# The router's logits of the values with the router weights stationary in three column groups

## The chip, the cores and the metric

One core of a Trainium2 chip runs the whole program. The time is what the device takes for one execution, in microseconds (us). TensorE is PE in the profile (PEld is its weight loads), VectorE is DVE, ScalarE is ACT, GpSimd is POOL, SyncE (which issues most DMAs) is SP.

## The reference

Three stages follow each other. (1) Attention in 16 heads (2 batches of 8) with 768 rows of 64 values, where a row attends only to the keys that have its own hash of six sign bits. (2) The 1536 rows of 512 values go through a mixture of 8 experts: each row goes to the expert with the largest logit, up to a capacity, and comes back weighted by its softmax probability. (3) A dense pair of layers with a hard swish between them. Cut to what matters here:

```
attn = softmax(where(mask, q @ k.T / 8, -1e9));  a = attn @ v          # 16 heads
x = a, heads side by side                                              # 1536 x 512
logits = x @ w_gate                                                    # 1536 x 8
e = argmax(logits);  gate = softmax(logits)[e]
y = relu(x @ w1[e]) @ w2[e] * gate
out = (h * clip(h + 3, 0, 6) / 6) @ w_out,  h = y @ w_in
```

## The kernel before

**How the logits come about.** The kernel doesn't form `x @ w_gate`. For each head it multiplies the values with that head's 64 rows of `w_gate` first, and appends the 8 columns that come out (a high and a low float16 half) to the values. The attention product then yields the 64 outputs and that head's share of the 8 logits at once. The function `vgate(r)` makes these columns for the pair of heads 2r and 2r+1, so it runs eight times, r = 0 to 7. Below, "product r" is its work on PE.

**What product r does.** The tile `vt` (loaded by `load_vt`, L526, one buffer) holds the values of the pair transposed: 128 partitions (two heads by 64) by 768 rows. For each of the six blocks of 128 rows, the block of `vt` is the stationary operand and the 16 columns of the weights (two heads by 8) are the moving one (L537). The result has the rows on the partitions. The program shows each such float32 product as two loads and two matmuls, so a pair has 12 of each. DVE then makes the two halves for each head (L546 and L547), into the tile `vh`.

**The loop.** The attention runs as 96 steps k, six for a head (one for each block of 128 keys), software-pipelined: step k makes the scores of block k on PE (L445, L446), their exponentials on ACT (L447), the float16 halves of block k-2 (L455 on ACT or L457 on DVE, L461 mostly on POOL), and the row maxima of block k+8 (L428 on PE, then two reductions of 384 columns on DVE, L431; the tile pool behind them has three banks of PSUM). In each odd step PE also multiplies two blocks of exponentials with the values (L473 to L475, 36 matmuls, the lines of `psv`). Every engine works through its instructions in the order in which the program text emits them.

**Small work between the steps.** All else hangs in a table of due times. `at(k, f)` puts a function at time k; `spread(k, gen, d)` runs a generator part by part, at k, k+d, k+2d and so on. Within step k, whatever is due up to k-0.5 is emitted ahead of the step's own work, and whatever is due up to k behind it; parts due at the same place go in order of their times. The table `Q` holds the times. `vgate` has two empty parts ahead of its matmuls, so they stand two parts after its start.

**One bank for the small products.** `misc()` hands out one PSUM bank (pool `ps_x`, one buffer) to everything small: the hash bits of the heads (`bits`, four matmuls of 32 columns each into four column groups, L401, and then the signs on DVE, L390), the scale of the values (`vscale`, L569 to L606, which in its first call also takes the maximum of the router weights, L571, and scales them, L605), the router's own counts, and `vgate`. A new user waits until the last reader of the one before is done.

**Around it.** SP issues the DMAs in the order of the program: loads of heads, copies of their halves into the operand tiles, the hash bits (L386), `vt`. After the loop come the routing (mostly small DVE work in a row), the experts (L1038, L1065) and the dense layers (L1287, L1314).

Of the kernel before, what the change touches and what calls it, by code (L numbers as in the profile page):

```python
# [9 lines left out]
F32 = mybir.dt.float32  # L10
# [9 lines left out]
P = 128  # L20
# [3 lines left out]
NC = S // P  # L24
# [3 lines left out]
KD = DM // P  # L28
E = 8
# [34 lines left out]
def moe_attention_kernel(ctx, tc, qk, v, vt, pj, wg, w1, w2, win, wout, out, cap):  # L64
    nc = tc.nc
    pe, act, dve, pool, sp = nc.tensor, nc.scalar, nc.vector, nc.gpsimd, nc.sync
# [16 lines left out]
    def persist(shape, dt, name):  # L83
        return const.tile(shape, dt, tag=name, name=name)
# [3 lines left out]
    ident = persist([P, P], F32, "ident")  # L88
# [6 lines left out]
    iota_s = persist([P, NS], F32, "iota_s")  # L95
    tokid = persist([P, NS], F32, "tokid")
    rank8 = persist([P, E], F32, "rank8")
    wg_sb = persist([P, KD, 2, E], F32, "wg_sb")
    isw = persist([P, 1], F32, "isw")
    lg = persist([P, B, NC, E], F32, "lg")  # L100
    ids = persist([P, E, NW], I32, "ids")
# [197 lines left out]
                )  # L299


    Q = {'v': (-3.25, -4.75, -1.75, -2.25), 'vg': (-4.5, -4.75), 'vgd': 1, 'pr': (-13.0, -12.75, -12.0, -12.5), 'prd': 0.6, 'b0': 7.75, 'b': 1.75, 'bd': 0.5, 'vm0': (8.0, 8.25, 10.75, 13.0), 'vm': (-0.5, 4.75, 7.0, 12.25), 'vs': 13.25, 'pa': 1.5, 'ev': 0.5, 'lvt': -5.0, 'v4': (2.0, 3.75, 4.0, 16.25), 'vg0': (1.85, -4.4, 7.75), 'p2': 3.5, 'lr': (0, 3, 1.5, 4.5), 'lv': 5.5, 'vsd': 0.75, 'ac': (0, 0, 2, 6, 7, 8, 9, 10), 'hd': (3, 5, 17), 'hn': (1, 3, 2, 0, 2, 0, 0, 0), 'ap': (0,), 'h0': (7,), 'hl': (4, 7, 10), 'l0': (), 'll': (1,), 'ht': (6, 3, 7, 6, 3, 2)}


    HT = Q["ht"]
# [1 line left out]
    with ExitStack() as actx:  # L307
# [220 lines left out]
        def vgate(r):  # L528

            sw = sw_t[r // 2]  # L530
            t = vt_t.pop(r)
            yield
            yield
            ps = misc(f"psg{r}")
            w = wg_sb[:, r % KD].rearrange("p h e -> p (h e)")
            for j in range(NC):
                pe.matmul(  # L537
                    ps[:, j * 2 * E : (j + 1) * 2 * E], t[:, j * P : (j + 1) * P], w, start=True, stop=True
                )
            yield  # L540
            ps = ps[:, 0 : NC * 2 * E].rearrange("p (c h e) -> p c h e", h=2, e=E)
            for hh in range(2):
                h = 2 * r + hh
                t = vh(h)
                o, ol = hh * D, VA + hh * D
                dve.tensor_scalar(out=t[:, :, o : o + E], in0=ps[:, :, hh], scalar1=sw, scalar2=None, op0=ALU.mult)  # L546
                dve.scalar_tensor_tensor(  # L547
                    out=t[:, :, ol : ol + E], in0=ps[:, :, hh], scalar=sw, in1=t[:, :, o : o + E],
                    op0=ALU.mult, op1=ALU.subtract,
                )  # L550
                yield
# [68 lines left out]
        def unmatched(r):  # L620

            b, k = divmod(r, KD)
            rows = rows_of(r)
            n = 2 * NC * D
            vt = pr.tile([P, S], F32, tag="r", name=f"uv{r}").rearrange("p (h c d) -> p h c d", h=2, c=NC)
            sp.dma_start(out=vt.rearrange("p h c d -> p (h c d)"), in_=v[:, r * n : (r + 1) * n])
            last = r == NH // 2 - 1
            if not last:
                x = pr.tile([P, S], F32, tag="r", name=f"ux{r}").rearrange("p (c d) -> p c d", c=NC)
                sp.dma_start(out=x, in_=rows)  # L630
            m = pt.tile([P, S], F32, tag="pf", name=f"um{r}", bufs=4)
            ps = misc(f"psu{r}")
            for c in range(NC):
                pe.matmul(ps[:, 0:P], ones, vt[:, :, c], start=c == 0, stop=c == NC - 1)
            act.activation(m[:, 0:P], ps[:, 0:P], AF.Copy, scale=1.0 / S)
            ps = misc(f"psc{r}")
            pe.transpose(ps[:, 0:P], m[:, 0:P], ident)
            act.activation(m[:, P : 2 * P], ps[:, 0:P], AF.Copy, scale=SW)
            ps = misc(f"psl{r}")
            pe.matmul(  # L640
                ps[:, 0 : 2 * E], m[:, P : 2 * P], wg_sb[:, k].rearrange("p h e -> p (h e)"), start=True, stop=True
            )
            z = nm[:, 2 * r : 2 * r + 2].rearrange("p h c -> p c h")
            y = pt.tile([P, S], F32, tag="pf", name=f"uy{r}", bufs=4).rearrange("p (c h d) -> p c h d", c=NC, h=2)
            dve.tensor_tensor(
                out=y, in0=bc(z, D), in1=mid(m[:, 0:P].rearrange("p (h d) -> p h d", h=2), NC), op=ALU.mult
            )
            if last:

                x = xp_t[r][:, :, E : E + D]  # L650
                dve.tensor_tensor(out=x, in0=x, in1=y[:, :, 0], op=ALU.add)
                sp.dma_start(out=rows[:, :, 0:D], in_=x)
                x = pv_t[2 * r + 1][:, 0 : NC * VA].rearrange("p (c d) -> p c d", d=VA)
                t, n = y[:, :, 1], nm[:, 2 * r + 1]
                dve.tensor_scalar(
                    out=t, in0=t, scalar1=sc_t[r // 2][:, 0:1], scalar2=float(S), op0=ALU.mult, op1=ALU.mult
                )
                dve.tensor_tensor(out=x[:, :, 0:D], in0=x[:, :, 0:D], in1=t, op=ALU.add)
                dve.scalar_tensor_tensor(
                    out=x[:, :, DE], in0=n, scalar=float(S), in1=x[:, :, DE], op0=ALU.mult, op1=ALU.add  # L660
                )
            else:
                dve.tensor_tensor(out=x, in0=x, in1=y.rearrange("p c h d -> p c (h d)"), op=ALU.add)
                sp.dma_start(out=rows, in_=x)
            y = pt.tile([P, S], F32, tag="pf", name=f"uz{r}", bufs=4)[:, 0 : NC * 2 * E]
            y = y.rearrange("p (c h e) -> p c h e", c=NC, h=2)
            dve.tensor_tensor(
                out=y, in0=bc(z, E), in1=mid(ps[:, 0 : 2 * E].rearrange("p (h e) -> p h e", h=2), NC), op=ALU.mult
            )
            for hh in range(2):  # L670
                dve.tensor_tensor(out=lg[:, b], in0=lg[:, b], in1=y[:, :, hh], op=ALU.add)
# [102 lines left out]
        def spread(k, gen, d=1):  # L774


            def part(k):
                if next(gen, gen) is not gen:
                    n = k + (d if k < STEPS - NC * 2 else min(d, 1) * 0.75)
                    at(n, part, n)  # L780

            at(k, part, k)
# [18 lines left out]
        for h in range(NH):  # L801
            k = NC * h + NC - 1 + LAG
            if h < NH - 1:
                at(k + Q["ev"], evac, h)
            if h % 2 == 0:
                if h:
                    spread(Q["vg0"][2] if h == 2 else NC * h + Q["vg"][h % 4 // 2], vgate(h // 2), Q["vgd"])
            elif h < NH - 1:
                at(k + Q["pa"], pair, h // 2)
                at(NC * h + Q["lvt"], load_vt, h // 2 + 1)  # L810
# [701 lines left out]
```

## Time and profile before

| what | value |
|---|---|
| median of 3 runs | 667.53 us (665.48, 667.53, 670.2) |
| the profiled execution, its own time | 666.91 us |
| its span, first to last instruction | 665.2 us |
| busy share of the span | PE 96%, PEld 72%, DVE 72%, ACT 64%, POOL 34% |
| mean granted TensorE clock | 0.985 of full speed |

The time of the profiled execution is 1.7 us more than its span, and 0.62 us less than the median of the runs. "Busy" counts the time in which an engine had an instruction under way; matmuls overlap each other, so that the busy time of PE says less than the distance from one instruction's start to the next one's. Times in rows of the trace count from the start of the span.

### The profile page before, as it was taken

The numbers are of one execution on the slowest core, as the hardware profiler recorded it, in microseconds if no ns is written. First come the engines' busy times: TensorE is split into PE (matmuls) and PEld (weight loads), VectorE is DVE, ScalarE is ACT, GpSimd is POOL, SyncE is SP. The second block draws the span as 40 slices with busy tenths as digits, with TensorE's granted clock in tenths as the row PEclk, the third lists the DMA queues.
The fourth block names the chain that finished last, engine by engine and source line by source line (L and its number), as shares of the span: only waits on it lengthen the run. The fifth ranks groups of instructions, "written<-read, shape, count | busy, mean of one in ns | idle before, by whom it ended". The sixth has DMA issues, their size and how long they took to land.

```text
span 665.2 us, 14405 instructions
## 1 busy us (share of the span) xinstructions
PE 635.3 (96%) x5534; PEld 479.4 (72%) x5534; DVE 478.9 (72%) x1041; ACT 425.3 (64%) x867; POOL 226.5 (34%) x198
## 2 busy tenths in 40 slices
PE   6899999999999879999999999999999999999893
PEld 2689888889898749999999996555555555555541
DVE  6778888898999888888888887888888342222320
ACT  2668878778787747777667765544555586555830
POOL 5357869769778133121366500000000021000011
PEclk8989999999999899999999999999999999999998
DMA  8685764774464339877677733444441010000011
GB/s 240 144 227 136 239 171 125 219 182 119 102 175 154 101 100 316 265 242 241 216 255 252 235 117 99 154 148 138 152 134 64 1 63 33 1 0 1 1 49 52
DMA packets 38642, 94.14 MB, mean 142 GB/s; under 512 B 9146, under 2 KB 14522, under 8 KB 38562
## 3 DMA queue, kind: packets, MB, share of 16 engines
q1 hardware_dynamic: 35474, 85.71, 43.1%
q0 software_dynamic: 2400, 7.36, 3.2%
q8 instruction: 46, 0.75, 0.5%
q14 instruction: 34, 0.28, 0.1%
q10 hardware_dynamic: 688, 0.03, 0.1%
HBM read 67.14 MB, written 6.29 MB: 110 GB/s over the span
## 4 chain that ended last, share of the span: by engine, by line
PE 55%; ACT 3%; DMA 2%; DVE 2%; issue 1%; POOL 0%; POOLq 0%; DVEq 0%
PE psg L1287 16%; PE pso L1314 15%; PE psy L1065 11%; PE psh L1038 11%; DMA out_dram<-os,inv 2%; ACT junk L1241 1%; PE psa L1015 1%; ACT gh L1297 1%; DVE rl L1290 1%; ACT rl L1289 0%; PE heat L1117 0%; DVE wl L164 0%; POOL out_dram L1329 0%; PE psw L296 0%; DVE os L1321 0%
## 5 line engine op out<-in xcount | busy, mean ns | idle before, releaser
L461 POOL TENSOR_TENSOR plo<-pf,phi 128x768 f16<-128x768 f32 x85 | 145.0, 1732 | 45.1 <-ACT phi L455 21.4
L447 ACT ACTIVATE pf<-pst 128x384 f32<-128x384 f32 x192 | 83.4, 486 | 44.5 <-PE pst L446 41.2
L431 DVE TENSOR_REDUCE mx<-psm 128x1 f32<-128x384 f32 x192 | 96.3, 548 | 21.5 <-PE psm L428 21.3
L1329 POOL DMA_INDIRECT out_dram<-os,inv x12 | 12.2, 1014 | 270.6 <-DVE os L1321 244.3
L164 DVE SCALAR_TENSOR_TENSOR wl<-raw,wh 128x1024 f16<-128x1024 f32 (+1 forms) x68 | 83.2, 1227 | 5.9 <-ACT wh L158 5.2
L1287 PE MATMUL psg<-yTh,ch 128*128 128x512 f16 (+1 forms) x256 | 83.4, 326 | 3.2 <-DVE rl L1290 3.2
L1287 PE MATMUL psg<-yTl,ch 128*128 128x512 f16 (+1 forms) x256 | 83.4, 326 | 0.0
L1287 PE MATMUL psg<-yTh,cl 128*128 128x512 f16 (+1 forms) x256 | 83.4, 326 | 0.0
L1290 DVE SCALAR_TENSOR_TENSOR rl<-rl,psg 128x512 f32<-128x512 f32 x64 | 35.0, 550 | 64.5 <-ACT rl L1289 64.0
L445 PE MATMUL pst<-Y,K 128*128 128x384 f32 x192 | 75.4, 393 | 1.8 <-ACT pf L447 1.7
L1287 PEld LDWEIGHTS <-ch 128*128 128x128 f16 x512 | 50.1, 98 | 35.9
L1314 PE MATMUL pso<-ch,gh 128*128 128x512 f16 x192 | 72.8, 379 | 0.0
L1314 PE MATMUL pso<-ch,gl 128*128 128x512 f16 x192 | 72.8, 379 | 0.0
L1314 PE MATMUL pso<-cl,gh 128*128 128x512 f16 x192 | 72.8, 379 | 0.0
L455 ACT ACTIVATE phi<-pf 128x768 f16<-128x768 f32 x83 | 70.0, 844 | 1.9
L428 PE MATMUL psm<-K,X 76*128 76x384 f32 x192 | 65.8, 421 | 4.7 <-DMA X<-b 2.1
L1314 PEld LDWEIGHTS <-gh 128*128 128x128 f16 x384 | 37.6, 98 | 42.3
L158 ACT ACTIVATE wh<-raw 128x1024 f16<-128x1024 f32 (+1 forms) x68 | 67.6, 998 | 0.5 <-issue 0.5
L1065 PE MATMUL psy<-hh,wl 128*128 128x224 f16 x256 | 66.3, 259 | 0.0
L1065 PE MATMUL psy<-hh,wh 128*128 128x224 f16 x256 | 66.3, 259 | 0.0
L1065 PE MATMUL psy<-hl,wh 128*128 128x224 f16 x256 | 66.3, 259 | 0.0
L446 PE MATMUL pst<-X,K 77*128 77x384 f32 x192 | 66.1, 344 | 0.0
(231 smaller groups left out, 1494.6 us busy)
## 6 DMA issues: line engine op xcount, KB each, us to landing
raw<-in_w_dram SPq DMA_DIRECT2D x64, 512.0 KB
rc<-in_win_dram SPq DMA_DIRECT2D x16, 512.0 KB
rc<-in_wout_dram SPq DMA_DIRECT2D x16, 512.0 KB
r<-in_qk_dram SPq DMA_DIRECT2D x16, 384.0 KB
K<-hi SPq DMA_DIRECT2D x31, 192.0 KB
vr<-in_v_dram SPq DMA_DIRECT2D x4, 768.0 KB
vt<-in_vt_dram SPq DMA_DIRECT2D x8, 384.0 KB
Y<-hi SPq DMA_DIRECT2D x16, 192.0 KB
```

Of the source, the lines that this page charges most:

```text
L158: act.activation(wh[e, i][:, c : c + n], r, AF.Copy, scale=(S1, S2)[i // 2])
L164: dve.scalar_tensor_tensor(out=wl[e, i][:, c : c + n], in0=r, scalar=(S1, S2)[i // 2], in1=wh[e, i][:, c : c + n], op0=ALU.mult, op1=ALU.s ...
L431: dve.tensor_reduce(out=mm[:, c, n : n + 1], in_=ps[:, :HS], axis=AX.X, op=ALU.max)
L445: pe.matmul(ps[:, :HS], st["K1"][:, kc], st["Y"][:, qc], start=True, stop=False)
L446: pe.matmul(ps[:, :HS], st["K2"][0:77, kc], st["X"][0:77, qc], start=False, stop=True)
L447: act.activation(pf.rearrange("k (c n p) -> k c n p", c=NC, n=2)[:, :, n], ps[:, :HS].rearrange("k (p c) -> k c p", c=NC), AF.Exp, scale=0 ...
L455: act.activation(phi_t[k], pf_t[k], AF.Copy)
L461: eng.tensor_tensor(out=plo_t[k], in0=pf_t.pop(k), in1=phi_t[k], op=ALU.subtract)
L1038: pe.matmul(ps, l[:, c], r[:, k], start=n == 0, stop=n == 3 * KD - 1)
L1065: pe.matmul(ps, l, r, start=n == 0, stop=n == 3 * KF - 1)
L1287: pe.matmul(ps, l, x, start=n == 0, stop=n == 3 * KD - 1)
L1314: pe.matmul(po[blk][s], l, r, start=first and n == 0, stop=last and n == 2)
```

## The change

The weights become the stationary operand: 32 columns (four slots of 8, of which two are used and two are zero), in three column groups of the array, and each group gets a third of `vt`, 256 columns, as the moving operand. The result has the logits on 96 partitions and the rows along the free dimension. DVE copies it to SBUF (tile `gv`, 96 by 256), and PE turns it back with two transpositions of 96 by 128 into another part of the same PSUM bank. The two parts that make the halves read from there. `vgate` so has two parts more (copy, transpositions), and its start is set two steps sooner, from -4.5 and -4.75 to -6.5 and -6.75 before its pair's first step; product 1 starts at 8.0 with a distance of 0.75 between parts, instead of 7.75 with 1. The weights' tile grows to four slots, which the first `vscale` reads and scales.

```
-    wg_sb = persist([P, KD, 2, E], F32, "wg_sb")
+    wg_sb = persist([P, KD, 4, E], F32, "wg_sb")
-    Q: 'vg': (-4.5, -4.75), 'vg0': (1.85, -4.4, 7.75)
+    Q: 'vg': (-6.5, -6.75), 'vg0': (1.85, -4.4, 8.0)
             ps = misc(f"psg{r}")
             w = wg_sb[:, r % KD].rearrange("p h e -> p (h e)")
-            for j in range(NC):
+            for i in range(3):
                 pe.matmul(
-                    ps[:, j * 2 * E : (j + 1) * 2 * E], t[:, j * P : (j + 1) * P], w, start=True, stop=True
+                    ps[32 * i : 32 * i + 32, 0 : 2 * P], w, t[:, 2 * i * P : (2 * i + 2) * P], start=True, stop=True
                 )
             yield
-            ps = ps[:, 0 : NC * 2 * E].rearrange("p (c h e) -> p c h e", h=2, e=E)
+            gv = ph.tile([96, 2, P], F32, tag="gv", name=f"gv{r}")
+            dve.tensor_copy(gv, ps[0:96, 0 : 2 * P].rearrange("p (m k) -> p m k", m=2))
+            yield
+            ps = ps[:, 2 * P : 2 * P + 192]
+            for m in range(2):
+                pe.transpose(ps.rearrange("p (i m x) -> p m i x", i=3, m=2)[:, m], gv[:, m], ident[0:96, 0:96])
+            yield
+            ps = ps.rearrange("p (c h e) -> p c h e", h=4, e=E)
             for hh in range(2):
...
-                ps[:, 0 : 2 * E], m[:, P : 2 * P], wg_sb[:, k].rearrange("p h e -> p (h e)"), start=True, stop=True
+                ps[:, 0 : 2 * E], m[:, P : 2 * P], wg_sb[:, k, 0:2].rearrange("p h e -> p (h e)"), start=True, stop=True
...
-                    spread(Q["vg0"][2] if h == 2 else NC * h + Q["vg"][h % 4 // 2], vgate(h // 2), Q["vgd"])
+                    spread(Q["vg0"][2] if h == 2 else NC * h + Q["vg"][h % 4 // 2], vgate(h // 2), 0.75 if h == 2 else Q["vgd"])
```

The line at L641, with `[:, k, 0:2]`, belongs to a branch that runs only when a row has no key with its hash.

## Rows read from the trace of the kernel before

**Rows 1.** Busy time of each engine by stretch: us, engines with counts, PEclk, DMA share, GB/s.

```profile
19.00:44.00 25.00, 22.92 (x174) 18.32 (x168) 17.60 (x43) 16.89 (x31) 12.12 (x7) 0.93 0.85 225
44.00:163.00 119.00, 117.07 (x1413) 105.24 (x1409) 102.91 (x234) 94.27 (x175) 94.78 (x62) 1.00 0.61 166
163.00:211.00 48.00, 47.06 (x584) 43.00 (x583) 44.42 (x106) 38.54 (x75) 38.23 (x26) 1.00 0.58 160
211.00:247.00 36.00, 29.75 (x387) 22.46 (x384) 31.20 (x94) 22.53 (x48) 9.14 (x9) 0.95 0.28 80
```

**Rows 2.** Waits of PE, then DVE, 44 to 163 us: total us, times, longest.

```profile
PE psm L428 <- DVE mx L431: 1.3, 4, 0.3
...
DVE mx L431 <- PE psm L428: 10.9, 16, 1.3
```

**Rows 3.** Timeline of PE around product 2: start, us, what, count.

```profile
72.45 0.20 PE L475 MATMUL psv<-vh,plo 128*128 128x73 f16 x1
72.49 1.49 PE L537 MATMUL psg<-wg_sb,vt 128*128 128x16 f32 x12
73.82 0.42 PE L445 MATMUL pst<-Y,K 128*128 128x384 f32 x1
```

**Rows 4.** Timeline of PE around a group of hash-bit products, and two passes of another.

```profile
138.91 0.20 PE L475 MATMUL psv<-vh,plo 128*128 128x73 f16 x1
139.04 0.85 PE L401 MATMUL psb<-r,pj_sb 128*32 128x384 f32 x8
139.82 0.44 PE L445 MATMUL pst<-Y,K 128*128 128x384 f32 x1
...
43.23 0.53 PE L401 MATMUL psb<-r,pj_sb 128*32 128x384 f32 x4
43.58 0.51 PE L401 MATMUL psb<-r,pj_sb 128*32 128x384 f32 x4
```

**Rows 5.** Timeline of PE around the transpositions of an expert's rows, and one alone.

```profile
263.76 0.60 PE L1015 MATMUL psa<-ident,xg 128*128 128x128 f32 x4
264.20 0.26 PE L1065 MATMUL psy<-hh,wh 128*128 128x224 f16 x1
...
57.67 0.27 PE L577 MATMUL psn<-ident,am 128*1 128x128 f32 x1
```

**Rows 6.** The hash bits' signs by line (ns min/median/max), scaling of the weights.

```profile
L390 DVE TENSOR_SCALAR b<-psb,pj_sb x8: 601/612/618, 19.5 to 140.0; 128x384 fp32r<-128x384 f32 x8
...
19.27 0.24 DVE L605 TENSOR_SCALAR wg_sb<-wg_sb,sc 128x64 f32<-128x64 f32 x1
```

**Rows 7.** Timeline of the first steps, where PE waited for a DMA.

```profile
33.69 0.77 PE L428 MATMUL psm<-K,X 76*128 76x384 f32 x2 [2.07 <-DMA X<-b]
```

**Rows 8.** Timelines around product 1: PE, then DVE.

```profile
47.39 0.44 PE L445 MATMUL pst<-Y,K 128*128 128x384 f32 x1
48.66 1.41 PE L537 MATMUL psg<-wg_sb,vt 128*128 128x16 f32 x12
49.92 0.42 PE L445 MATMUL pst<-Y,K 128*128 128x384 f32 x1
...
47.53 0.62 DVE L390 TENSOR_SCALAR b<-psb,pj_sb 128x384 fp32r<-128x384 f32 x1 [0.35 <-PE psb L401]
```

**Rows 9.** Timeline of DVE before product 2 and before product 6, and of PE.

```profile
69.93 1.02 DVE L431 TENSOR_REDUCE mx<-psm 128x1 f32<-128x384 f32 x2 [0.17 <-PE psm L428]
71.23 1.02 DVE L431 TENSOR_REDUCE mx<-psm 128x1 f32<-128x384 f32 x2 [0.27 <-PE psm L428]
...
174.97 1.94 DVE L431 TENSOR_REDUCE mx<-psm 128x1 f32<-128x384 f32 x4
...
177.21 1.48 PE L537 MATMUL psg<-wg_sb,vt 128*128 128x16 f32 x12
```

**Rows 10.** The last load of `vt` on SP, and PE at the start of step 80.

```profile
190.06 0.52 SPq L526 DMA_DIRECT2D vt<-in_vt_dram  x1
...
198.01 0.42 PE L445 MATMUL pst<-Y,K 128*128 128x384 f32 x1
```

More of the change, by code (lines that the diff above doesn't have):

```diff
@@ L299, in windows @@
                 )
-    Q = {'v': (-3.25, -4.75, -1.75, -2.25), 'vg': (-4.5, -4.75), 'vgd': 1, 'pr': (-13.0, -12.75, -12.0, -12.5), 'prd': 0.6, 'b0': 7.75, 'b': 1.75, 'bd': 0.5, 'vm0': (8.0, 8.25, 10.75, 13.0), 'vm': (-0.5, 4.75, 7.0, 12.25), 'vs': 13.25, 'pa': 1.5, 'ev': 0.5, 'lvt': -5.0, 'v4': (2.0, 3.75, 4.0, 16.25), 'vg0': (1.85, -4.4, 7.75), 'p2': 3.5, 'lr': (0, 3, 1.5, 4.5), 'lv': 5.5, 'vsd': 0.75, 'ac': (0, 0, 2, 6, 7, 8, 9, 10), 'hd': (3, 5, 17), 'hn': (1, 3, 2, 0, 2, 0, 0, 0), 'ap': (0,), 'h0': (7,), 'hl': (4, 7, 10), 'l0': (), 'll': (1,), 'ht': (6, 3, 7, 6, 3, 2)}
+    Q = {'v': (-3.25, -4.75, -1.75, -2.25), 'vg': (-6.5, -6.75), 'vgd': 1, 'pr': (-13.0, -12.75, -12.0, -12.5), 'prd': 0.6, 'b0': 7.75, 'b': 1.75, 'bd': 0.5, 'vm0': (8.0, 8.25, 10.75, 13.0), 'vm': (-0.5, 4.75, 7.0, 12.25), 'vs': 13.25, 'pa': 1.5, 'ev': 0.5, 'lvt': -5.0, 'v4': (2.0, 3.75, 4.0, 16.25), 'vg0': (1.85, -4.4, 8.0), 'p2': 3.5, 'lr': (0, 3, 1.5, 4.5), 'lv': 5.5, 'vsd': 0.75, 'ac': (0, 0, 2, 6, 7, 8, 9, 10), 'hd': (3, 5, 17), 'hn': (1, 3, 2, 0, 2, 0, 0, 0), 'ap': (0,), 'h0': (7,), 'hl': (4, 7, 10), 'l0': (), 'll': (1,), 'ht': (6, 3, 7, 6, 3, 2)}
     HT = Q["ht"]
```

## The prediction

> **What bounds the kernel now.** I read the busy times by stretch first: the change touches the attention loop alone, so the rest of the span matters only as far as it starts earlier or later. From 44 to 163 us PE has an instruction under way in 117.07 of 119 us, at the full clock, against 102.91 on DVE [rows 1]. The waits say who holds up whom there: DVE stands 10.9 us waiting for PE's score products, PE 1.3 us for DVE's reductions [rows 2]. So PE is the bound in that stretch, and what is taken off PE shortens it. From 163 to 211 us the routing of the first batch adds work on DVE: 44.42 of 48 us there are busy (93%), beside PE's 47.06 [rows 1]. Here the two are about level. From 211 to 247 us neither is full (PE 29.75 and DVE 31.20 of 36), since chains of small routing instructions set the pace; a shift of what comes before passes through. Before 44 us a DMA decides: at 33.69 PE has waited 2.07 us for a load of hash bits [rows 7].
>
> **What a product costs on PE now.** The distance between starts counts, not the sum of durations. Product 2 starts at 72.49, 0.04 behind the matmul before it, and the scores follow at 73.82: 1.33 us [rows 3]. Product 1 takes 49.92 - 48.66 = 1.26 us [rows 8].
>
> **What it costs after.** The nearest row for the new matmuls is the hash-bit group: four matmuls with 32 stationary columns and 384 moving ones, in four column groups. From the matmul before it to the scores behind it, it takes 139.82 - 138.91 = 0.91 us, or 0.87 without the usual 0.04 [rows 4]. That includes a later start, 0.13 instead of 0.04, and a gap behind it. Its eight instructions run as two passes of four side by side: four start together at 43.23, four at 43.58 [rows 4]. A pass of 384 columns so takes 0.35 us, 0.9 ns a column. The new group has 256 columns: 128 fewer in each of two passes, 0.23 us less, which gives 0.64 us. The bounds are 0.58 (two thirds of everything) and 0.87 (nothing shrinks). I take 0.64, because the columns of a pass are what is cut.
>
> The two transpositions are nearest to those of an expert's rows: four in 264.20 - 263.76 = 0.44 us, so 0.11 each and 0.22 for two [rows 5]. The bounds are 0.17 (96 of 128 columns) and 0.54 (the 0.27 us that a lone one lasts, twice [rows 5]). I take 0.22: the two stand back to back, as those four do. [...] The rows show both numbers: 0.27 is how long one lasts, 0.11 is the distance to the next. [...]
>
> A product so costs 0.64 + 0.22 = 0.86 us instead of 1.33 and **gains 0.47 us** (between +0.58 and, with both upper bounds, -0.08).
>
> **What it adds on DVE.** One copy of 256 columns from PSUM for each product. The signs read 384 columns from PSUM in 0.612 us [rows 6]; two thirds of that is 0.41 us. The parts that make the halves keep their place and shape. From 44 to 163 us DVE has 16.1 us free [rows 1] and four or five copies need 2.0, so cover is there. The copy delays the reductions behind it by up to 0.41 us, but before product 2 DVE waited 0.27 us for PE at that very place [rows 9].
>
> **Does PE wait for the copy?** The copy of product 2 stands behind the reductions that end at 69.93 + 1.02 = 70.95, so it is done by 71.36; PE comes to the transpositions where the old product stood, at 72.49 [rows 9, 3]. That leaves 1.1 us. Before product 6 the copy goes between the second and third of four reductions from 174.97 on, is done by about 176.35, and PE comes at 177.21 [rows 9]: 0.86 us are left. No wait, then, but the margin is one or two DVE instructions.
>
> **Product by product.** *Product 0:* its matmuls shrink in the first step, and the halves come one step later, but PE waits 2.07 us for hash bits at 33.69 [rows 7]; what is won or lost before goes into that wait. Nothing. The scaling of the doubled weights tile does lie on the way to those bits: DVE runs it, and the maximum over the same tile, ahead of the signs. 64 more elements at the signs' 1.6 ns are 0.1 us each (no more than the 0.24 us of the whole scaling [rows 6]): **+0.2**.
>
> *Product 1:* here the new due times add a wait. The second group of hash-bit signs is due at 9.25, and the matmuls move from 9.75 to 9.5, so from the end of step 10 to its start, right behind those signs, and both use the one bank that `misc` hands out. PE would start at 47.39, but the signs last from 47.53 to 48.15 [rows 8]: PE stands for 0.76 us. Queued behind it are the scores of step 10, and ACT's exponentials and DVE's maxima of that step wait with them. 0.76 + 0.86 - 1.26 = **+0.36**. The bank is held two parts longer in the other products too, but by the due times no user falls inside those parts.
>
> *Products 2 to 5:* the full gain four times, **-1.88**. *Products 6 and 7:* DVE is 93% busy there and gets 0.41 us more each time, so between 0 and 0.47 comes through; I take 0.2 each, **-0.4**.
>
> The loads of `vt` keep their place on SP and wait for a buffer that is now read sooner. The tightest is the last: issued at 190.06, needed at the start of step 80, 198.01 [rows 10], 7.95 us for 384 KB; at the 160 GB/s of that stretch [rows 1] that is 2.4 us of transfer (an estimate). ACT and POOL get nothing new, and SP issues what it did.
>
> **The sum:** +0.2 + 0.36 - 1.88 - 0.4 = -1.7 us. Against the profiled execution's own 666.91 this is 665.2; that execution stands 0.62 below the median of the runs, 667.53, and from there it is 665.8. I name **665.5**.
>
> **The rivals.** *A, more comes through (0.20).* If products 6 and 7 gain in full and PE catches up on the wait at product 1, six times 0.47 and a gain of 0.4 at product 1 with the 0.2 of the weights give -3.0: 663.9 to 664.5. For it: before product 6 PE, not DVE, could run ahead once its matmuls are out of the busiest step. Against it: 93% on DVE.
>
> *B, the copy makes DVE the bound, and it gets slower (0.12).* Place: the two reductions of 384 columns behind each copy. PE needs the bank of a reduction three back, so a copy that finds DVE without slack stops L428 by its whole 0.41 us, and the saving on PE is then idle time. Six times 0.41, with 0.36 and 0.2 from above: +3.0, 669.9. It decides where PE's waits for L431 grow by more than 0.47 us a product. Against it are the 10.9 us of DVE's waiting [rows 2]; for it is the stretch from 163 us. [...]
>
> *C, the three groups don't run side by side (0.03).* Then six passes of 0.23 us, with 0.13 for the start and 0.22 for the transpositions, make 1.73 us, 0.4 more than now: six times that with 0.56 is +3.0, again 669.9. The two passes of four [rows 4] speak against it.
>
> **How the numbers follow.** My forecast has 0.62, and 0.03 is left for what I don't see. The granted clock was 0.93 from 19 to 44 us [rows 1], which is 1.7 us of loss; a lower stretch more or less moves any case by about as much. The forecast's own range, with the bounds of the prices, is 664 to 667.5. Taking in A whole and most of B gives **663.0 to 668.6**. This kernel's measurement can tell about 1%, 6.7 us, from no change, and no case reaches that: faster 0.03, same 0.94, slower 0.03.
>
> **What would show it.** L537's successor has 6 matmul rows for each product instead of 12, with two passes about 0.24 us apart, and the start of the next PE work 0.64 us on; two transposition rows take 0.22. The pair of steps with product 2 is 0.47 us shorter, DVE has eight copies of about 0.41, and at step 10 PE waits some 0.8 us for the signs (L390). Wrong would be: a PE wait ahead of the transpositions, PE waits for L431 well over 1.3 us from 44 to 163 (B), a group that takes over 0.87, or no wait at step 10.

## The result, and the profile after

The changed kernel takes **672.47 us** (median of 8 runs, 671.1 to 680.06) where the kernel before took 667.42 beside it: ratio 1.0086, interval 1.0058 to 1.0114. That is 5 us slower, and over the predicted range (663.0 to 668.6, forecast 665.5), though still within 1%. One execution of before_shift (2452 us, below) was in the slow state and is left out of its ratio.

The profiled execution was the longest of the eight, 680.06 us. It holds two VectorE instructions that took 4 to 5 us more than usual (below), so most rows come from a second profile of the same kernel, "again" here: 675.42 us, span 673.7, median of its runs 673.49. Behind `vgate` the line numbers are seven higher than before. Busy time by stretch of that execution, columns as in [rows 1], with one more stretch below:

```profile
19.00:44.00 25.00, 22.27 (x172) 16.26 (x166) 18.92 (x47) 17.01 (x31) 11.58 (x7) 1.00 0.83 218
44.00:163.00 119.00, 113.06 (x1335) 97.91 (x1335) 100.40 (x231) 89.88 (x166) 90.53 (x59) 0.97 0.59 159
163.00:211.00 48.00, 47.19 (x574) 41.77 (x573) 44.85 (x104) 39.29 (x74) 39.42 (x27) 1.00 0.57 145
211.00:247.00 36.00, 27.98 (x404) 22.38 (x401) 32.62 (x86) 25.10 (x54) 8.13 (x8) 0.97 0.31 104
...
50.30:57.10 6.80, 6.80 (x49) 5.53 (x50) 3.63 (x8) 4.06 (x7) 5.05 (x4) 0.50 0.01 2
```

These stretches don't hold the same work as before, since the steps come later: from 44 to 163 us there are 1335 matmuls instead of 1413, and the five products account for only 20 of the 78 (12 rows then, 6 and 2 now). What the rows show is that PE isn't full there any more (113.06 of 119 us) and that DVE isn't either (100.40); how much PE was relieved is read from the timelines below. In the last row the granted clock is 0.50 for 6.8 us with PE busy throughout, which costs up to half of them, 3.4 (an estimate).

Timelines of PE around product 2, which answer to [rows 3] and [rows 5]: the matmuls in step 19, the transpositions two steps on.

```profile
74.20 0.20 PE L475 MATMUL psv<-vh,plo 128*128 128x73 f16 x1
74.32 0.63 PE L537 MATMUL psg<-vt,wg_sb 128*32 128x256 f32 x6
74.88 0.44 PE L445 MATMUL pst<-Y,K 128*128 128x384 f32 x1
...
78.65 0.20 PE L475 MATMUL psv<-vh,plo 128*128 128x73 f16 x1
78.69 0.36 PE L546 MATMUL psg<-ident,gv 96*128 96x96 f32 x2
78.82 0.44 PE L445 MATMUL pst<-Y,K 128*128 128x384 f32 x1
```

The group takes 74.88 - 74.20 = 0.68, 0.64 without the usual 0.04: as predicted. The transpositions cost 0.13, not 0.22. The copies, answering to [rows 6], and the waits of 44 to 163 us, answering to [rows 2]:

```profile
L542 DVE COPY gv<-psg x8: 406/410/411, 22.2 to 206.2; 96x256 f32<-96x256 f32 x8
```

```profile
DVE mx L431 <- PE psm L428: 11.1, 17, 2.1
...
PE psm L428 <- DVE mx L431: 1.9, 6, 0.4
```

The copy takes the predicted 0.41. PE's waits for the reductions rise by 0.6 us there, over five products.

**Where the time is.** I compared the start of each of the 96 steps (the first L445 of a step) with the same start before. The table is worked out from the traces: how many us each stretch of steps became longer, and the whole span.

| kernel | steps 0-7 | 8-13 | 14-82 | 83-94 | 95 to end | span |
|---|---|---|---|---|---|---|
| changed, again | -1.2 | +6.2 | -1.2 | +2.0 | +2.7 | 673.7 |
| old_early | +1.1 | +3.3 | -2.1 | +1.3 | +0.5 | 669.3 |
| before_shift | -1.3 | +2.2 | +0.2 | -1.5 | +0.7 | 665.5 |
| new_late | +1.7 | +1.2 | +6.9 | +1.0 | +3.3 | 679.3 |
| pad | -1.1 | +2.1 | -0.5 | +1.8 | +0.9 | 668.5 |
| align | +0.1 | +4.3 | -0.2 | +2.0 | +0.8 | 672.1 |
| al_v | +1.8 | +2.2 | -3.3 | +2.4 | +3.8 | 672.0 |
| route_late | +0.1 | +1.6 | -2.0 | 0.0 | +1.4 | 666.2 |
| p1_mid | +0.4 | -0.5 | -3.7 | +2.3 | +1.4 | 665.1 |
| combo | +1.8 | -0.3 | -1.1 | 0.0 | +3.8 | 669.4 |
| np_before | -0.2 | +1.6 | -5.1 | -2.1 | +0.7 | 660.1 |
| np_after | -1.3 | +0.6 | -6.7 | -2.1 | +3.8 | 659.6 |
| np_align | +0.5 | +1.0 | -8.5 | -2.1 | +3.9 | 660.0 |

The kernels are those of the experiments. Up to step 13 the table says little of the change: the three other profiles with the old form (old_early, before_shift, np_before) differ there from the one of the kernel before by 0.9 to 4.4 us in all. In steps 91 to 93 the kernel before lost 0.9 + 0.4 + 0.3 us that the others don't, in a stretch at a granted clock of 0.51 (222.0 to 225.5 us), so +2.0 in steps 83 to 94 is a loss of some 3.6. The gain lies in steps 14 to 82, where six products were to give 0.2 to 0.47 each (-2.3); it came out at -1.2, and the rest lost more. From what repeats in most profiles one gets -1.2 + 3.6, and 1.7 for a branch behind the loop (below), or some 4 of the 5 us; this is an estimate from one profile of each kernel.

Product by product the gain is there. In the pair of steps of product 2, "again" needs 0.68 more in step 19 (matmuls) and 1.19 less in step 21: -0.52. Products 3 to 5 give as much (-0.52 to -0.53), and 6 and 7 give -1.05 and -1.12. Then it goes back: steps 24, 48 and 62 are 0.49 longer each, 72 0.68, 76 0.46, and 84, 85 and 87 1.35, 1.09 and 0.93. The same steps lose the same amounts in most kernels with the new form. At 24, 48, 62, 72, 84, 85 and 87 PE or its weight load waits for L431.

**What those steps hold.** Timelines of "again" (first fence), of DVE, POOL and PE, and of the kernel before (second) around its VectorE routing instructions L248 and L250:

```profile
210.10 4.89 POOL L461 TENSOR_TENSOR plo<-pf,phi 128x768 f16<-128x768 f32 x3
210.92 0.88 DVE L248 SCALAR_TENSOR_TENSOR pl<-mx,pos 128x6 f32<-128x6 f32 x1
211.72 1.70 DVE L250 SCALAR_TENSOR_TENSOR jt<-tokid,jo 128x24 f32<-128x24 f32 x1
213.35 1.01 DVE L431 TENSOR_REDUCE mx<-psm 128x1 f32<-128x384 f32 x2
213.95 0.56 PE L428 MATMUL psm<-K,X 76*128 76x384 f32 x1 [1.02 <-DVE mx L431]
...
217.78 1.66 POOL L461 TENSOR_TENSOR plo<-pf,phi 128x768 f16<-128x768 f32 x1 [2.79 <-PE psv L475]
218.17 1.29 DVE L277 TENSOR_SCALAR se<-se 128x6 f32<-128x6 f32 x1
```

```profile
206.50 0.29 DVE L248 SCALAR_TENSOR_TENSOR pl<-mx,pos 128x6 f32<-128x6 f32 x1
206.71 0.17 DVE L250 SCALAR_TENSOR_TENSOR jt<-tokid,jo 128x24 f32<-128x24 f32 x1
206.81 1.01 DVE L431 TENSOR_REDUCE mx<-psm 128x1 f32<-128x384 f32 x2
...
211.66 0.17 DVE L277 TENSOR_SCALAR se<-se 128x6 f32<-128x6 f32 x1
```

An instruction on 24 columns that took 0.17 us takes 1.70. The three subtractions of GpSimd lie back to back from 210.10 to 214.99, 1.63 us each in the mean, so the second goes from about 211.73 to 213.36 (an estimate); L250 starts at 211.72 and ends at 213.42. L277 ends at 219.46, POOL's subtraction at 219.44. **These VectorE instructions start here while GpSimd's subtraction is under way and don't end before it: L248 takes 0.88 us instead of 0.29, L250 1.70 and L277 1.29 instead of 0.17, and in the rows below L378 takes 1.58 instead of 0.95 and L693 2.04 instead of 0.61.** I call them held. Not every instruction is: the reductions L431, which read PSUM, took 0.54 to 0.56 us in all 192 cases of "again", beside a subtraction too. But they stand behind the held ones; so they are late, and PE waits 1.02 us for their bank. PE's waits for L431 from 163 to 230 us rise from 0.6 to 3.0 us. In the kernel before, DVE started first at that place, and it was GpSimd that took longer: L378 took its own 0.95 us from 40.28, and the subtraction from 40.69 took 2.05 instead of 1.65. PE shows no wait there, from 40.2 to 44 us. In "again" the order is turned:

```profile
39.54 1.65 POOL L461 TENSOR_TENSOR plo<-pf,phi 128x768 f16<-128x768 f32 x1 [0.25 <-POOL plo L461]
...
40.42 1.58 DVE L378 SCALAR_TENSOR_TENSOR lo<-r,hi 128x768 fp32r<-128x768 f32 x1 [1.21 <-DMA Y<-lo]
41.92 1.94 DVE L431 TENSOR_REDUCE mx<-psm 128x1 f32<-128x384 f32 x4
...
42.52 0.55 PE L428 MATMUL psm<-K,X 76*128 76x384 f32 x1 [0.61 <-DVE mx L431]
```

The rows show who waits and until when; what the two engines share, no row shows. The two long instructions in the 680.06 us execution are of such lines:

```profile
102.95 8.07 POOL L461 TENSOR_TENSOR plo<-pf,phi 128x768 f16<-128x768 f32 x5
105.92 5.52 DVE L693 SCALAR_TENSOR_TENSOR vh<-vr,sc,vh 128x384 f16<-128x384 f32 x1
...
212.54 6.50 POOL L461 TENSOR_TENSOR plo<-pf,phi 128x768 f16<-128x768 f32 x4
214.96 4.11 DVE L248 SCALAR_TENSOR_TENSOR pl<-mx,pos 128x6 f32<-128x6 f32 x1
```

Here the VectorE instruction isn't let in between two subtractions: it ends when a whole row of them ends (at 111.02, where L693 ends at 111.44, and at 219.04, where L248 ends at 219.07). In "again" L250 went on behind a single one. What decides between the two isn't shown.

**Product 1 and the start.** "again" waits for the second group of signs as forecast, but longer (1.28 us for L390, forecast 0.76), because DVE itself stood 2.62 us for the values' load:

```profile
46.48 1.01 DVE L567 TENSOR_REDUCE am<-vr 128x1 f32<-128x384 f32 x2 [2.62 <-DMA vr<-in_v_dram]
...
50.20 0.97 PE L537 MATMUL psg<-vt,wg_sb 128*32 128x256 f32 x6 [1.28 <-DVE b L390]
```

The stretch at a granted clock of 0.50 from 50.3 us begins behind these waits of PE. In the 680.06 us execution the sign wait is 0.74 and no such stretch follows (the granted clock is 1.00 from 44 to 60 us); the clock and the load differ from execution to execution. Such stretches aren't only there: of the profiles with products two steps sooner, the subtraction in place and the routing at 65 or 66, all but "again" and align have one of 3.4 us or more that begins in steps 83 to 86; in the 680.06 us execution the granted clock is 0.50 from 219.4 to 225.6 us. In al_v (below) the granted clock is 0.51 from 213.40 to 216.80, behind PE's waits of 1.02 and 0.98 us for L431, and step 85 loses 2.2 us where it loses 1.1 in "again". The wait at 33.69 [rows 7] stays: 1.98 us at 33.94.

**Behind the loop** a branch of PE ends later. Timelines around the first routing matmuls behind it, of the kernel before and of "again":

```profile
236.74 0.20 PEld L232 LDWEIGHTS <-ident 128*128 128x128 f16 x5 [1.83 <-PEq L856]
236.77 0.27 PE L232 MATMUL psr<-oh,ident 128*128 128x40 f16 x5 [1.36 <-DVE rs L227]
```

```profile
244.24 0.20 PEld L232 LDWEIGHTS <-ident 128*128 128x128 f16 x5 [3.48 <-PEq L863]
244.27 0.27 PE L232 MATMUL psr<-oh,ident 128*128 128x40 f16 x5 [3.02 <-PEq L863]
```

From the start of step 95 (229.43 and 235.26) these matmuls come 9.0 us later instead of 7.3. Before, they waited for DVE; now they wait for PE's own branch.

### The profile page after: what moved, and what is told of

The parts are those of the page before. It is cut to its first block, busy times and chain, and to the rows that moved or that the text cites. A ratio compares the mean times of both kernels' runs of the same rounds, so it can differ in the third digit from the quotient of the medians.

```text
span 678.3 us, 14350 instructions
## 1 busy us (share of the span) xinstructions
PE 638.6 (94%) x5502; PEld 475.6 (70%) x5502; DVE 490.1 (72%) x1049; ACT 425.5 (63%) x867; POOL 226.5 (33%) x198
## 4 chain that ended last, share of the span: by engine, by line
PE 55%; ACT 3%; DMA 2%; DVE 1%; issue 1%; POOL 0%; POOLq 0%
PE psg L1294 16%; PE pso L1321 15%; PE psy L1072 11%; PE psh L1045 11%; DMA out_dram<-os,inv 2%; ACT junk L1248 1%; PE psa L1022 1%; ACT gh L1304 1%; DVE rl L1297 1%; PE heat L1124 0%; ACT rl L1296 0%; DVE wl L164 0%; PE heatt L326 0%; POOL out_dram L1336 0%; DVE os L1328 0%
## 5 line engine op out<-in xcount | busy, mean ns | idle before, releaser
L431 DVE TENSOR_REDUCE mx<-psm 128x1 f32<-128x384 f32 x192 | 96.5, 549 | 22.4 <-PE psm L428 22.1
L428 PE MATMUL psm<-K,X 76*128 76x384 f32 x192 | 68.3, 429 | 12.9 <-DVE mx L431 9.0
L445 PE MATMUL pst<-Y,K 128*128 128x384 f32 x192 | 76.4, 398 | 1.9 <-ACT pf L447 1.8
L428 PEld LDWEIGHTS psm<-K,X 76*128 76x128 f32 x192 | 53.9, 313 | 21.6 <-DVE mx L431 14.4
L473 PE MATMUL psv<-vh,phi 128*128 128x73 f16 x576 | 67.2, 202 | 0.0
L474 PE MATMUL psv<-vh,phi 128*128 128x72 f16 x576 | 66.9, 203 | 0.0
```

Source lines behind the costliest of these rows:

```text
L428: pe.matmul(ps[:, :HS], st["X"][0:76, c::NC], st["K2"][0:76, n * HS : (n + 1) * HS], start=True, stop=True)
L431: dve.tensor_reduce(out=mm[:, c, n : n + 1], in_=ps[:, :HS], axis=AX.X, op=ALU.max)
L445: pe.matmul(ps[:, :HS], st["K1"][:, kc], st["Y"][:, qc], start=True, stop=False)
```

## The experiments

My theory at the start was that the saving on PE arrives, and is spent on meetings of DVE and GpSimd; the rivals were the copy as DVE's bound (B of the prediction), and a cost of the form itself. All ratios are to the kernel before, run beside it.

**1. again**: the changed kernel unaltered.

> The changed kernel once more, for a profile of an execution near its median (the first one took 680.06 us, with one VectorE instruction of 5.5 us and one of 4.1 us in it). Held-VectorE theory (each product saves its 0.5 us on TensorE, and the time is lost again where L378 or L693 on VectorE meet L461 on GpSimd, and at the wait of product 1): 671 to 673 us, the steps with the products 0.5 us shorter as in the first profile, and single steps behind them 0.5 to 1 us longer, each with a long L378 or L693. Dear-product theory (the products themselves cost more on TensorE): the steps of the products are longer than before.

1.0072 (1.0043 to 1.0101), 673.49 us. The loss is there again, with the rows above.

**2, 3. np_before, np_after**: the old and the changed kernel without GpSimd's subtraction; the low halves are zeros.

```
+            if eng is pool:
+                pf_t.pop(k)
+                plo_t[k] = nil      # zeros
+                return
             eng.tensor_tensor(out=plo_t[k], in0=pf_t.pop(k), in1=phi_t[k], op=ALU.subtract)
```

> The kernel before without the subtractions on GpSimd (L461): the low halves of the exponentials of those steps are zeros from a fixed tile, all matmuls stay. It is the base for np_after. Held-VectorE theory: L378 and L686 fall to about 1.0 us each, TensorE's waits shrink, 2 to 8 us faster than before. Dear-product theory: says nothing of it.

> The changed kernel, with the subtractions on GpSimd left out in the same way. Held-VectorE theory: nothing holds VectorE any more, so the saving of the products stays: 2 to 4 us under np_before. Dear-product theory (or a loss at the PSUM bank alone): 3 to 6 us above np_before, as the changed kernel stands to the one before.

0.9889 (0.9850 to 0.9929) and 0.9884 (0.9845 to 0.9923). Lengths of the split of the values by line (ns: min/median/max), in "again", then in np_after:

```profile
L693 DVE SCALAR_TENSOR_TENSOR vh<-vr,sc,vh x16: 608/874/2041, 20.8 to 225.7; 128x384 f16<-128x384 f32 x16
```

```profile
L699 DVE SCALAR_TENSOR_TENSOR vh<-vr,sc,vh x16: 606/608/614, 20.8 to 210.5; 128x384 f16<-128x384 f32 x16
```

Every one now takes 0.61 us. The new form is no longer slower, so what made it slower needs the subtraction. (PE needs the subtraction's result, too, but in neither the profile of the kernel before nor in "again" does a PE instruction of the loop wait for GpSimd; so it isn't a late operand.) Up to step 95 np_after is 3.6 us ahead of np_before (-9.4 against -5.8). Each of products 2 to 7 gains 0.53 to 0.56 there, 6 and 7 too: their 1.1 above was half a hold of the kernel before. In steps 14 to 82 as a whole np_after is only 1.5 us ahead, since steps 14, 48, 76 and 78 lose 0.48, 0.28, 0.53 and 0.26, without any subtraction: at 14 PE waits for the small products' bank (L590 behind L582), at 48 and 78 for a DMA. So the loss at 14 isn't a hold. But the whole time doesn't show those 3.6 us: the last stretch takes 3.1 more, of it 2.4 behind the last matmul, where the output's scatter waits for its DMAs.

**4. pad**: each pair of transpositions of products 1 to 7 issued four times.

```
-            for m in range(2):
+            for m in range(2) if r == 0 else [0, 1] * 4:
```

> The changed kernel with each pair of transpositions (but that of product 0) issued four times, so that TensorE does about 0.5 us more for each of seven products, nearly what a product cost before. Held-VectorE theory: TensorE's saved time was lost anyway, so the added 3.4 us come to 1 us or less, or even gain. Dear-product theory (TensorE's work sets the time): 3 to 4 us above the changed kernel.

1.0065 (1.0039 to 1.0092), no slower than without it.

```profile
74.67 0.85 PE L546 MATMUL psg<-ident,gv 96*128 96x96 f32 x8
75.31 0.44 PE L445 MATMUL pst<-Y,K 128*128 128x384 f32 x1
```

75.31 - 74.67 = 0.64 instead of 0.13: 0.5 us of PE seven times, 3.5 us, and nothing is lost in the time. The losses at steps 24, 48 and 62 are gone instead, so that 2.9 us of added work come to 0.7 in steps 14 to 82. Two things go with it: a product costs PE nearly what the old one did, and still steps 83 to 87 lose 3.6 us, so that loss doesn't come from shorter products; and pad has 42 more matmuls ahead of the branch, which isn't late here (experiments 9 and 10). PE's time alone doesn't set the end here.

**5. p1_back**: product 1 due as before, 7.75 with distance 1.

> The changed kernel with product 1's due times as before (start 7.75, parts 1 apart), so that its matmuls stand at the end of step 10, behind the hash bits' signs. Held-VectorE theory: TensorE no longer stands for the signs at steps 9 to 11 (0.66 us more there than before in the first profile), 0.5 to 1.5 us under the changed kernel, still 3 to 4 us over the one before. Bank theory (the one PSUM bank at product 1 is what costs): 4 to 5 us under the changed kernel, as the one before.

1.0096 (1.0074 to 1.0119). The loss moves: step 9 loses 0.35 instead of the 1.38 of the changed kernel's first profile, but steps 14 to 16 lose 3.0 instead of 0.7, with the granted clock at 0.51 from 60.8 to 64.2 us. The 0.5 to 1.5 us expected under the changed kernel didn't come.

**6. act_copy**: the copy to SBUF on ACT, where it takes 0.38 us.

> The changed kernel with the copy of the turned products on ScalarE (ACTIVATE, copy) instead of VectorE, in the same place of the order. Copy theory (the 0.41 us on VectorE make it the bound, eight times): 3 us or more under the changed kernel. Held-VectorE theory: VectorE's instructions only come 0.4 us sooner there and meet other GpSimd subtractions; within 1.5 us of the changed kernel.

1.0079 (1.0047 to 1.0111): the same as with DVE's copy, and not the 3 us or more faster of the copy theory. Rival B falls.

**7, 8. old_early, new_late**: the old form two steps sooner, and the new form at the old times.

```
-    'vg': (-4.5, -4.75)      old_early
+    'vg': (-6.5, -6.75)
-    'vg': (-6.5, -6.75)      new_late (product 1 as in p1_back)
+    'vg': (-4.5, -4.75)
```

> The kernel before (values stationary, 12 matmuls) with products 2 to 7 begun two steps sooner, nothing else. Move theory (the two steps alone cost): 3 to 5 us over the kernel before. Held-VectorE theory: TensorE's work is as before, only 1.3 us of it stand two steps sooner; the meetings change for better or worse, within 2 us of the kernel before.

> The new form at the old start times (products 2 to 7 at -4.5 and -4.75, product 1 at 7.75 with 1 apart): matmuls where they stood, transpositions and halves two steps later. Move theory: the loss is gone, at or under the kernel before. Held-VectorE theory: TensorE saves the same 0.5 us per product, and the time given back depends on which VectorE instructions meet a subtraction; 0 to 5 us over the kernel before, with long L378, L693 or routing instructions in the steps that lost.

1.0020 (0.9991 to 1.0049) and 1.0176 (1.0159 to 1.0194). The earlier start alone costs nothing that can be told (up to 3.3 us stay possible). Its profile shows that it deals the holds anew by itself: steps 83 to 87 lose 3.1 us with the old form too, while 25 and 49 gain 0.57 and 0.59. So the loss there goes with the earlier start and not with the new form; in old_early gains of 2.1 us in steps 14 to 82 stand against it.

new_late, at 12 us over the kernel before, lies outside what either theory allowed. Without the earlier start steps 14 to 82 lose 6.9 us, and not by holds alone: PE stands for the halves, the last to read the small products' bank. Waits of PE, 20 to 240 us:

```profile
PE psn L584 <- DVE vh L554: 2.4, 3, 1.5
PE psb L401 <- DVE vh L554: 2.4, 2, 1.4
```

In "again" PE has no such wait.

**9, 10. align, before_shift**: PE's instruction stream made longer, to see whether the late branch behind the loop goes with the number of PE instructions ahead of it. The change took 32 matmuls out; that 96 more would act in the old kernel as 32 fewer was my assumption, which no run ahead of these shows. In align 11 filler matmuls of 512 columns are each cut into 4 of 128 in the changed kernel; in before_shift 16 are cut into 7 of 73 in the old one.

```
-                pe.matmul(heat_t[pool_][:, :cols], ...)
+                for _ in range(m):      # 4 for the first 11; 7 for the first 16
+                    c = cols // m
+                    pe.matmul(heat_t[pool_][:, :c], ...)
```

> The changed kernel with 33 more matmuls on TensorE in its first steps: eleven of the 512-column filler matmuls (L326) are cut into four of 128 columns, so that TensorE has as many instructions ahead of the branch behind the attention loop (L856 before, L863 after) as in the kernel before, and hardly more work. [...]

> The kernel before with 96 more matmuls of TensorE in its first steps (sixteen filler matmuls cut into seven of 73 columns). [...]

1.0077 (1.0047 to 1.0108) and 1.0047 (1.0019 to 1.0075). Waits around that branch, 222 to 248 us, in align and then in before_shift:

```profile
PEld L232 <- PEq L870: 1.7, 1, 1.7
PE psr L232 <- ACT ex L272: 1.3, 1, 1.3
```

```profile
PEld L232 <- PEq L863: 3.0, 1, 3.0
PE psr L232 <- PEq L863: 2.6, 1, 2.6
```

33 more matmuls (with their loads) in PE's stream take the late branch out of the changed kernel, 96 put it into the old one: from step 95 the matmuls come 7.3 and 8.6 us later. In these traces it goes with the number of PE instructions ahead: in all profiles with 2487 or 2615 matmuls ahead of L232 it comes 8.6 to 9.0 us behind step 95, in all with 2519 to 2529 it comes 7.2 to 7.6. Why it goes with that number is shown by no run. The time of align doesn't show those 1.7 us, though; that of before_shift rose by 3.1 (1.3 to 5.0), which the branch may or may not explain.

**11, 12. al_v, al_pr**: align with one phase moved: the split of every fourth head (L693) a step later, or one group of DVE's preparations a quarter of a step sooner.

```
-    'v': (-3.25, ...)           -    'pr': (-13.0, ...)
+    'v': (-2.25, ...)           +    'pr': (-13.25, ...)
```

> align, with the values' split of every fourth head (L693 of heads 4, 8, 12) a step later, away from the start of the subtraction on GpSimd that it meets in the changed kernel. Held-VectorE theory: the 0.5 to 0.7 us lost at steps 24, 48 and 72 are gone or stand elsewhere; 0.5 to 1.7 us under align if gone, and L693 of heads 4 and 8 no longer 2.04 us. Rival (those steps are slow for another reason): the same losses at the same steps.

> align, with the preparation of every fourth head a quarter step sooner, which puts its L378 ahead of the reductions of its step instead of behind them. Held-VectorE theory: the 0.3 to 0.5 us lost at steps 14, 38 and 62 are gone or stand elsewhere, and L378 of those heads no longer lasts 2.3 us; up to 1 us under align. Rival: the same losses at the same steps.

1.0030 (1.0000 to 1.0060) and 1.0060 (1.0035 to 1.0084). DVE at the place of the loss at step 24, in "again" and in al_v:

```profile
79.36 6.80 POOL L461 TENSOR_TENSOR plo<-pf,phi 128x768 f16<-128x768 f32 x4
81.00 2.04 DVE L693 SCALAR_TENSOR_TENSOR vh<-vr,sc,vh 128x384 f16<-128x384 f32 x1
```

```profile
78.49 9.17 POOL L468 TENSOR_TENSOR plo<-pf,phi 128x768 f16<-128x768 f32 x5
81.52 0.65 DVE L700 SCALAR_TENSOR_TENSOR vh<-vr,sc,vh 128x384 f16<-128x384 f32 x1
```

The same split takes 2.04 us in one and 0.65 in the other. In "again" it starts at 81.00, about where the second of the four subtractions does (79.36 and one of 1.65, an estimate); in al_v it starts at 81.52 and isn't held, and the row of five subtractions that it falls in takes 9.17 us instead of 8.25, five times 1.65. Steps 24 and 48 no longer lose 0.49, but gain 0.08 to 0.09, and 25 and 49 gain 0.56 and 0.58; the 0.68 of step 72 goes too, but 73 loses 0.90. Steps 14 to 82 come to -3.3. In al_pr the losses at 14, 38 and 62 go, and 37 and 61 lose 0.7; its longest L378 is 1.92 us instead of 2.30.

**13. np_align**: align without the subtraction.

> align without the subtractions on GpSimd (as in np_before and np_after: those low halves are zeros). Both causes of the loss are then out of the way. [...] If a third cause of a microsecond or more is left: 0.987 or above.

0.9909 (0.9878 to 0.9939), above the 0.987 from which a third cause was to be left. (np_before's 0.9889 less the products' 3.2 us would have been 0.984, an estimate.) In the loop the products gain 0.53 to 0.56 each, as in np_after, and steps 14 to 82 are 3.3 us ahead of np_before, against six times 0.54 = 3.2; in np_after they were 1.5. (In np_align step 14 loses its 0.48 again, and a wait of np_before for a DMA at step 24, 0.67, isn't there.) Again the end takes it back (+3.9 against +0.7), here with the early branch. Of it some 0.8 lies ahead of the last matmul, where PE waits longer for the experts' gathered rows, and 2.3 behind it, in the output's scatter. Scatter of np_before, then np_align:

```profile
648.80 0.96 POOL L1335 DMA_INDIRECT out_dram<-os,inv  x1 [2.60 <-DMA out_dram<-os,inv]
652.75 0.96 POOL L1335 DMA_INDIRECT out_dram<-os,inv  x1 [2.98 <-DMA out_dram<-os,inv]
```

```profile
648.89 0.96 POOL L1349 DMA_INDIRECT out_dram<-os,inv  x1 [4.79 <-DMA out_dram<-os,inv]
652.73 0.96 POOL L1349 DMA_INDIRECT out_dram<-os,inv  x1 [2.88 <-DMA out_dram<-os,inv]
```

Two executions of the changed kernel differ by 1.3 us behind the last matmul, so it need not be the change's; what decides it stays open.

**14, 15. route_early, route_late**: al_v with the routing of block 0 spread from 65 or 67 instead of 66.

> al_v with the routing of the first batch started a step sooner (at 65 instead of 66), so that its small instructions L248 and L250 come at other places against GpSimd's subtractions. Held-VectorE theory: the 3 to 4 us lost at steps 83 to 87 change with it, to 0 to 3 us; no more L250 of 1.7 us. Rival (those steps lose for another reason, such as the transpositions of product 7 in front of them): the same loss at the same steps.

> al_v with the routing of the first batch started a step later (at 67). Held-VectorE theory: as for route_early, the loss at steps 83 to 87 changes, up or down, with the instructions that meet a subtraction. Rival: the same loss at the same steps.

1.0105 (1.0068 to 1.0142) and 1.0043 (1.0015 to 1.0070). In route_late L250 takes 0.17 us again, and steps 83 to 94 cost 0.0 instead of +2.4 (1.6 instead of 4.0 us, if the 1.6 that the kernel before lost in steps 91 to 93 is added to both). Not all of that is the holds: al_v has its 3.4 us at a granted clock of 0.51 there, and route_late none. Steps 75 and 77 now lose 0.99 and 0.42, and by the median route_late gained nothing over al_v. In route_early L250 still takes 1.69 us, against what was expected, steps 83 to 94 cost +2.0, and one split took 5.6 us.

**16. p1_mid**: al_v with product 1 due at 8.25 instead of 8.0, behind the second group of signs.

> al_v with product 1 started at 8.25 (0.75 between parts), so that its matmuls stand behind the hash bits' signs by a step's work, and its transpositions and halves a half step later. Forecast's term for the wait at product 1: the 0.7 us lost at steps 9 to 11 are gone, 0.5 to 1 us under al_v. Held-VectorE theory adds that other meetings behind it may take back as much.

1.0021 (0.9999 to 1.0042). PE at product 1, in the changed kernel's first profile and in p1_mid:

```profile
49.39 0.63 PE L537 MATMUL psg<-vt,wg_sb 128*32 128x256 f32 x6 [0.74 <-DVE b L390]
```

```profile
49.12 0.63 PE L544 MATMUL psg<-vt,wg_sb 128*32 128x256 f32 x6
```

The wait is gone, and steps 8 to 13 come to -0.5.

**17. combo**: p1_mid and route_late together.

> The new form with three phases set anew together: the split of every fourth head a step later, product 1 a quarter of a step later (both as in the version that measured 1.0021 to the kernel before) and the routing of block 0 one step later. In the version with routing at 66, steps 84 and 85 lose 1.3 and 2.2 us where VectorE's routing instructions start just behind GpSimd's subtraction; with routing at 67 those steps lost 0.7 and 0.9 instead. If these meetings set the time (theory), the gains add up: start of step 95 at about -3.4 us against the kernel before instead of -1.5, and the whole 0.998 to 1.000 of it. If what the new form costs is elsewhere (rival: its own price on PE or VectorE), the routing's place brings nothing and the time stays at 1.002 or above.

1.0008 (0.9984 to 1.0032). Steps 84 and 85 lose 0.0 and 0.75 instead of 1.35 and 2.2, as expected; 87 loses 0.88. Step 95 doesn't start at -3.4, though, but at +0.4: step 0 of this execution started 1.8 later, and step 26, where PE waited for a load of a head, lost 1.37. The new form with three phases set anew takes what the old kernel takes; none of these versions beats it.

## Why the prediction was wrong

**The prices held.** Matmuls 0.64 (forecast 0.64), transpositions 0.13 (0.22), copy 0.41 (0.41), gain per product 0.54 (0.47). One transposition by itself lasts 0.25 us (244 to 275 ns in "again"), and the two still cost 0.13 between other matmuls. Product 0 gave nothing, as said. No wait for the copy stands ahead of the transpositions at product 2, and rival C is out. Rival A had the products right: 6 and 7 gain in full, and not the 0.2 of the forecast, but the time didn't follow.

**Product 1** was right in place and price (a wait of 0.74 where 0.76 was forecast). It was too small where DVE is late for another reason: 1.28 in "again".

**The step that failed** is "So PE is the bound in that stretch, and what is taken off PE shortens it", with its cover, "ACT and POOL get nothing new". PE was busiest, but the pace there is that of a loop of PE, DVE and POOL. I read 16.1 us of free time on DVE as cover, and didn't look at what a DVE instruction costs by where it starts against the subtraction, although the trace before had L686 from 0.61 to 1.81 us and L378 from 0.95 to 2.04. An earlier product, its moved parts and its shorter time shift every later meeting. Instead of the -2.3 us forecast for products 2 to 7, steps 14 to 82 came to -1.2 and steps 83 to 87 lost 3.6. That the holds are behind it is shown in three ways: 3.5 us of added PE work cost nothing (pad), without the subtraction the new form isn't slower (np_after against np_before, 0.9884 and 0.9889), with a gain of 1.5 and 3.3 us in steps 14 to 82 (np_after, np_align), and moving one phase removes the losses at its places (al_v, route_late). The losses of steps 83 to 87 come with the earlier start alone (old_early), which the sum had at nothing. By the interval of old_early that start needn't make the whole slower; which of its holds come out as time differs with what else is shifted.

**Rival B** had the right sign and the wrong mechanism: PE does wait longer for L431 (0.6 to 3.0 us from 163 to 230), but the copy on ACT changes nothing. Its 669.9 was too little, too, beside 672.47.

**The tail** was costed at nothing ("a shift of what comes before passes through"). The matmuls behind the branch came 1.7 us later, with 2487 matmuls ahead of them in PE's stream instead of 2519. Its share of the median isn't settled.

**The clock** stood in the forecast as 1.7 us more or less in any case. It differs by kernel: the mean granted clock of the executions is 0.9840 in the six of "again" and 0.9895 in the fifteen of the kernel before beside them; for combo it is 0.9906, beside 0.9905. A share of 0.0055 of 672 us is 3.7 us of the 5, as an upper bound, since some of it can fall where PE waits anyway; this is an estimate. Some holds stand ahead of a stretch at about half the clock: in the 680.06 us execution PE waits 3.41 us for L431 behind the L693 of 5.52 us, up to 112.46, and the granted clock is 0.50 from 110.0 to 116.4. Whether such a hold brings the stretch on isn't shown; no run holds the clock fixed, and what each of the two costs isn't parted.

**Still open:** why 3 us won in the loop without the subtraction don't appear in the time, and how the changed kernel's 5 us divide between holds, clock and branch. What the three shifts together account for is 1.0077 to 1.0008, 4.6 us.

## What to carry to other kernels

Before moving or shortening a step, look at the spread of single instructions on VectorE while GpSimd is at work: a line of one shape with a minimum of 0.61 and a maximum of 1.81 us was held by something here, and every shift dealt those holds out anew. Judge cover by what happens when the two meet, not by an average of free time. After such a change set the phases of the held instructions again; here that was worth 0.7%, as much as the change had cost, and the same steps showed where.

## What the runs showed of the hardware

- While GpSimd's subtraction was under way, VectorE instructions that took 0.17 us before took 1.70 (L250) and, with a single SBUF operand, 1.29 (L277) in "again". Instructions of 5.52 (L693) and 4.11 us (L248) occurred in the 680.06 us execution, each until the end of a row of back-to-back subtractions. The reductions from PSUM (L431) took 0.54 to 0.56 us in all 192 cases.
- The matmuls behind a branch in PE's stream came 1.7 us later with 2487 matmuls ahead of them ("again") than with 2519 (the kernel before). The page of the profile lists an instruction queue (q8) with 46 packets and 0.75 MB; that the branch waits for one of them is shown by no run.
- Two transpositions of 96 by 128 cost 0.13 us of PE between other matmuls, and three column groups of 256 columns 0.56 to 0.64 ("again", product 2).
